# An adaLN block in fp32: down weights asked for earlier, joining sums and the last rows' projection moved

## The chip, the cores and the metric

The kernel runs on one core of a Trainium2 chip. That core has TensorE (PE, with its weight loads shown as PEld), VectorE (DVE), ScalarE (ACT), GpSimd (POOL) and SyncE (SP, here only a queue of DMA requests). All five run their own instruction streams in the order in which they were written down, and wait for one another through semaphores. The metric is device time of one execution in microseconds (us). Before the change the median of three runs is 2881.68 us.

## The reference

One transformer block with adaptive layer norm, in fp32. There are 2048 rows of 576 features, 32 heads of 18 features and a gated feed-forward part of 4608 features.

```python
mod = (silu(c) @ w_mod).reshape(1, 6, 1, -1)
sa, ca, ga, sb, cb, gb = (mod[:, i] for i in range(6))

h = layernorm(x) * (1 + ca) + sa
q, k, v = heads(h @ wqkv)                  # 32 heads of 18
p = softmax(q @ k.T * 18**-0.5)            # 2048 x 2048 for each head
x = x + ga * (merge(p @ v) @ wo)

h = layernorm(x) * (1 + cb) + sb
x = x + gb * ((sigmoid(h @ w_gate) * (h @ w_up)) @ w_down)
```

## The kernel before, in words

**Attention.** The 2048 query rows are two halves. A unit is a pair of heads for one half, so there are 32 units, and each has 16 steps, one for every 128 keys. In a step PE makes four tiles of scores, ACT turns them into exponentials, and PE multiplies these with the values, two steps behind, into one sum bank `o` (L577). Between them PE makes a second set of scores in turns ("m" in the order strings), from which DVE takes the row maxima (L481) that a later unit needs. The maxima run about a unit and a half ahead and end during unit 30. In a paired unit ACT takes over a part of the maxima (L484, L486). In the units listed in `SINGLE` DVE reduces all of them.

The end of a unit is handed on in three places of the next unit. At its step 1 ACT copies the bank `o` into the tile `oT` (L591). At step 3 PE transposes `oT`, DVE takes reciprocals and ACT writes the transposed tile back into `oT` (L616). Then POOL scales it into the output rows `Oa` or `big` (L620). There is one `oT` and one bank `o`, so the copy of the next unit waits until POOL has read the last one, and PE's next values wait for that copy.

**Work beside attention.** Three generators are advanced a piece at a time.

- `down_parts` prepares the 18 blocks of down weights on POOL, from unit 4, step 8 to unit 14, three pieces in four steps. For each block it asks for the weights (L852, a POOL DMA tied to an exponential of that step), scales them by the gate (four L873), makes the sums for a seven-product matrix scheme (L879 to L883), splits everything into a high and a low part (L869, L870, L898, L899) and stores it to DRAM (L892 for the parts, L900 twice for the sums). Two weight tiles alternate.
- `first_rows` projects the first half of the rows, from unit 15 on.
- `last_rows_project` projects the second half in eight groups of 128 rows, from unit 27, step 5 on. Each group takes three turns, one in every second step: transposes, then nine matmuls for each of two column halves (L714), with a DVE addition (L716). Its rows of x arrive by POOL DMA in a tile of the feed-forward pool (`raw1`), where the sums are also made and stored from.

Units 16 to 20 and 27 to 29 run with `SINGLE` maxima. From unit 1 to unit 29 SP asks, at the start of a unit, for the queries and keys of the unit after next (L440 to L448), eight requests.

The order of PE's instructions is written out by hand in all of this. The order on the other engines is set by a planner, which places an instruction where its own estimate says that the engine is free and the inputs are there. It places the code's instructions, and the code's order only breaks ties.

**Feed-forward.** Each half of the rows goes through 18 blocks of 256 hidden features. A block takes seven products, in the order 1, 6, 2, 7, 5, 4, 3, and two half "downs" with the weights prepared above. In the second half, blocks 1 to 16 also use the seven-product scheme for the down part: products go into four tiles `G`, and in the last block eight joining sums (`joined`, L1243) add these to the output. From the seventh product on DVE and ACT keep the code's order too.

Of the kernel before, what the change touches and what calls it, by code (L numbers as in the profile page):

```python
# [15 lines left out]
F32 = mybir.dt.float32  # L16
F32R = mybir.dt.float32r
# [6 lines left out]
P = 128  # L24
S = 2048
D = 576
# [11 lines left out]
HW = S // 2  # L38
UNITS = H
LEAD = 6  # L40
FROM0, FROM1 = 15 * 16, 27 * 16 + 5
DL = 384
ORDER = (1, 6, 2, 7, 5, 4, 3)
LOOK = 4
# [1 line left out]
NB = F // 256  # L46
LAG = 2

MAXIMA = ((1, 0), (0, 0), (1, 1), (0, 2), (1, 2), (0, 3), (0, 1), (1, 3))
SINGLE = (0, 1, 16, 17, 18, 19, 20, 27, 28, 29)  # L50
FIRST = ((0, 0), (1, 0), (0, 2), (0, 1), (1, 1), (1, 2), (0, 3), (1, 3))
STARTS = tuple(range(2, 15))
STARTED = ((0, 0), (0, 1), (1, 1), (1, 0)), ((0, 0), (0, 1), (1, 0), (1, 1))
# [10 lines left out]
def tile_block(ctx, tc, x_in, wqkv, wo, w_gate, w_up, w_down, c_in, w_mod, out):  # L64
# [351 lines left out]
    def temp(shape, dtype):  # L416
        temps["n"] += 1
        return qpool.tile(shape, dtype, name=f"t{temps['n'] % 2}")
# [213 lines left out]
    def load_wo():  # L632
# [31 lines left out]
        for _ in range(4):  # L664
            yield

    def project_o(t):

        wo_h, wo_l, we = weights
        T, T_ = temp([P, 2048], F32R), temp([P, 2048], F32)  # L670
        xt, full, od = T_[:, 0:D], T_[:, 1024:1536], T_[:, 1536:1664]
        if t >= 8:
            xt = raws.tile([P, 2, 3, 256], F32, name="raw1", bufs=2).rearrange("p v t c -> p (v t c)")[:, 0:D]
        nc.gpsimd.dma_start(xt, x_rows[:, t, :])
        src = Os[t // 8][:, t % 8, :]
        n = 4 if t < 8 else DL // P
        oh = T[:, 0 : n * P]
        ol = T[:, 512 : 512 + n * P]
        pt = bank()
        for i in range(n):  # L680
            nc.tensor.transpose(pt[:, i * P : (i + 1) * P], src[:, i * P : (i + 1) * P], ident)
        if t >= 12:
            nc.vector.tensor_copy(oh, pt[:, 0 : n * P])
            nc.vector.tensor_sub(ol, pt[:, 0 : n * P], oh.bitcast(F32))
        else:
            full = full[:, 0 : n * P]
            nc.vector.tensor_copy(full, pt[:, 0 : n * P])
            nc.gpsimd.tensor_copy(oh, full)
            nc.gpsimd.tensor_sub(ol, full, oh.bitcast(F32))
        yield  # L690
        if t < 8:
            om = T[:, 1024:1152]
            omh = T[:, 1152:1280]
            nc.gpsimd.tensor_copy(
                od.rearrange("p (a e) -> p a e", e=64), src[:, DM:D].unsqueeze(1).to_broadcast([P, 2, 64])
            )
            pt = bank()
            nc.tensor.transpose(pt[:, 0:P], od, ident)
            nc.vector.tensor_copy(od, pt[:, 0:P])
            nc.gpsimd.tensor_copy(om[0:64], od[0:64])  # L700
            nc.gpsimd.tensor_copy(omh[64:P], od[64:P])
            nc.gpsimd.tensor_sub(om[64:P], od[64:P], omh[64:P].bitcast(F32))
            yield
        for h in range(2):
            cols = slice(h * HALF, (h + 1) * HALF)
            ts_ = []
            for i in range(n):
                a, b = oh[:, i * P : (i + 1) * P], ol[:, i * P : (i + 1) * P]
                ts_ += [(a, wo_h[:, i, cols]), (a, wo_l[:, i, cols]), (b, wo_h[:, i, cols])]
            if t < 8:  # L710
                ts_ += [(om, we[:, 0, cols]), (om, we[:, 1, cols])]
            acc = bank()
            for i, (a, w) in enumerate(ts_):
                nc.tensor.matmul(acc[:, :HALF], a, w, start=i == 0, stop=i == len(ts_) - 1)  # L714
            to = Oa[:, t, :] if t < 8 else xt
            nc.vector.tensor_add(to[:, cols], xt[:, cols], acc[:, 0:HALF])  # L716
            yield
        if t >= 8:
            nc.gpsimd.dma_start(x1p[:, t - 8, :], xt)
# [128 lines left out]
    def down_parts():  # L848
# [9 lines left out]
        ahead = load(0)  # L858
        yield
        yield  # L860
        for b in range(NB):
            t = ahead
            hi, lo = t[:, 0 : 2 * D], t[:, 2 * D : 4 * D]
            raw = lo.bitcast(F32)
            quads = [slice(i * HALF, (i + 1) * HALF) for i in range(4)]
            b11, b12, b21, b22 = (raw[:, q] for q in quads)

            def split(i):
                nc.gpsimd.tensor_copy(hi[:, quads[i]], raw[:, quads[i]])  # L869
                nc.gpsimd.tensor_sub(lo[:, quads[i]], raw[:, quads[i]], hi[:, quads[i]].bitcast(F32))  # L870

            for i, q in enumerate(quads):
                nc.gpsimd.tensor_mul(raw[:, q], raw[:, q], gb_b[:, i % 2 * HALF : (i % 2 + 1) * HALF])  # L873
                if i == 2:
                    yield
            if b < SEVENS:
                two = [temp([P, 2048], F32R) for _ in range(2)]
                (t1, t2), (t3, t4) = ([x[:, (2 + i) * HALF : (3 + i) * HALF].bitcast(F32) for i in range(2)] for x in two)
                nc.gpsimd.tensor_sub(t1, b12, b11)  # L879
                nc.gpsimd.tensor_sub(t3, b22, b12)  # L880
                yield
                nc.gpsimd.tensor_sub(t2, b22, t1)
                nc.gpsimd.tensor_sub(t4, t2, b21)  # L883
            if b + 1 < NB:
                ahead = load(b + 1)
            yield
            split(0)
            split(1)
            yield
            split(2)  # L890
            split(3)
            nc.gpsimd.dma_start(wds[b].bitcast(F32), t[:, 0 : 4 * D].bitcast(F32))  # L892
            yield
            if b < SEVENS:
                for i, x in enumerate(two):
                    for k in range(2):
                        to, part = x[:, k * HALF : (k + 1) * HALF], x[:, (2 + k) * HALF : (3 + k) * HALF]
                        nc.gpsimd.tensor_copy(to, part.bitcast(F32))  # L898
                        nc.gpsimd.tensor_sub(part, part.bitcast(F32), to.bitcast(F32))  # L899
                    nc.gpsimd.dma_start(  # L900
                        wtd[b, :, 2 * D * i : 2 * D * (i + 1)].bitcast(F32), x[:, 0 : 2 * D].bitcast(F32)
                    )
                    yield
# [558 lines left out]
    for n, (hf, b, k) in enumerate(seq):  # L1462
# [72 lines left out]
        if k == 1:  # L1535
# [6 lines left out]
            flush()  # L1542
            if hf and not b:
                second_half()
        elif k == 6:
            st["b_"] = banks()
            product(st, 6, st["b_"], True)
# [44 lines left out]
                behind.append(got)  # L1592
        if hf and not b and k in (4, 3):
            load_columns(0, {4: 2, 3: 4}[k])
        if hf and b == NB - 1:
            for i in {1: (0, 1), 2: (2, 3), 5: (4,), 4: (5, 6), 3: (7,)}.get(k, ()):
                joined(i)
        if before is not None and k == 6:
            down(before, 0, {3: lambda: weights_low(n + 2)})
        elif before is not None and k == 7:  # L1600
            down(before, 1, {3: lambda: weights_low(n + 2), 5: lambda: weights_low(n + 3), 7: lambda: weights_low(n + 4)})
        elif k in (6, 7):
            for i in (2,) if k == 6 else (2, 3, 4):
                weights_low(n + i)
# [56 lines left out]
```

## Time and profile before

| | |
|---|---|
| median of three runs | 2881.68 us (2878.94 to 2881.8) |
| the profiled execution | 2879.64 us, span 2877.8 us |
| granted PE clock, mean | 0.996 |
| attention, units 0 to 31 | 242.8 to 1601.3 us of the span |
| feed-forward | 1606.2 us to the end |

A profile lists, for each engine, when it was busy and what ended its idle time. PE is busy for 98% of the span, and this counts matmuls whose ends are modelled, so it doesn't mean that PE could not do more. The lines that carry the argument are shown with the prediction. In a timeline a row gives start, length, engine, line, operation, tiles written and read, shapes and how many instructions were merged. The bracket holds the engine's idle time before it and what ended that.

### The profile page before, as it was taken

What the parts mean: (1) busy time and instruction counts of PE and PEld (TensorE: products, weight loads), DVE (VectorE), ACT (ScalarE), POOL (GpSimd) and SP (SyncE); (2) the same over time, 40 slices, a digit from 0 to 9 for tenths busy, and PEclk for the clock granted to TensorE, in tenths of its full rate; (3) what the DMA queues carried; (4) which work ended last, traced back from release to release, by engine and by line L of the source; (5) the groups of instructions that cost most, each with busy time, mean ns of one, the idle gap of its engine ahead of it and who ended that gap; (6) DMA issues with size and microseconds to landing.
All of it is one profiled execution on the core that took longest, in us unless ns stands there. A gap on an engine that the chain in (4) does not pass through costs nothing.

```text
span 2877.8 us, 46834 instructions
## 1 busy us (share of the span) xinstructions
PE 2820.3 (98%) x16885; PEld 1855.6 (64%) x16885; DVE 2336.0 (81%) x4367; ACT 1591.6 (55%) x2989; POOL 821.3 (29%) x1089
## 2 busy tenths in 40 slices
PE   7999999999999999999999999999999999999998
PEld 5974444443434444444444688888888888888888
DVE  7287888888889998999985588887888687777776
ACT  2215899999988778998778522334333222222221
POOL 3125307776763111555012322232222100000000
PEclk9999999999999999999999999999999999999999
DMA  5444214444442111222124766667776966665653
GB/s 168 127 148 132 69 49 149 143 159 164 168 151 80 57 35 49 75 95 78 52 65 124 260 230 238 226 225 252 277 263 237 381 198 200 199 199 198 199 197 109
DMA packets 170104, 462.33 MB, mean 161 GB/s; under 512 B 21196, under 2 KB 87760, under 8 KB 159760
## 3 DMA queue, kind: packets, MB, share of 16 engines
q1 hardware_dynamic: 148768, 358.36, 37.0%
q0 software_dynamic: 21104, 100.98, 9.9%
q8 instruction: 133, 2.18, 0.3%
q14 instruction: 99, 0.81, 0.1%
HBM read 281.92 MB, written 176.82 MB: 159 GB/s over the span
## 4 chain that ended last, share of the span: by engine, by line
PE 83%; POOL 6%; DVE 4%; issue 3%; ACT 2%; DMA 1%; SPq 0%; POOLq 0%; ACTq 0%; DVEq 0%
PE x L1113 26%; PE o L577 14%; PE s L475 10%; PE s L985 10%; PE d L1263 8%; PE d L1195 6%; PE s L300 4%; PE s L714 2%; PE s L351 2%; ACT p L989 2%; POOL w L870 1%; POOL t L899 1%; DVE mx L481 1%; POOL w L873 1%; PE s L601 1%
## 5 line engine op out<-in xcount | busy, mean ns | idle before, releaser
L481 DVE TENSOR_REDUCE mx<-s 128x1 f32<-128x512 f32 x1696 | 1076.7, 684 | 128.5 <-PE s L475 110.2
L989 ACT ACTIVATE p<-s 128x512 f32<-128x512 f32 x2048 | 1068.7, 610 | 143.8 <-PE s L475 73.7
L475 PE MATMUL s<-k,q 54*128 54x512 f32 x1920 | 607.6, 451 | 8.3 <-ACT p L989 1.8
L577 PE MATMUL o<-p,vaug 128*32 128x512 f32 x4096 | 555.4, 608 | 6.9 <-ACT oT L591 6.5
L985 PE MATMUL s<-q,k 56*128 56x512 f32 x1920 | 555.4, 426 | 1.7 <-DVE mx L481 0.6
L985 PEld LDWEIGHTS s<-q,k 56*128 56x128 f32 x1920 | 264.9, 186 | 293.3 <-DVE mx L481 177.3
L475 PEld LDWEIGHTS s<-k,q 54*128 54x128 f32 x1920 | 272.8, 185 | 250.4 <-ACT p L989 150.4
L1113 PE MATMUL x<-k,w 128*128 128x512 f32 x1512 | 369.7, 392 | 2.4 <-ACT w L1094 2.4
L1113 PEld LDWEIGHTS x<-k,w 128*128 128x128 f32 x1512 | 278.3, 189 | 54.6 <-ACT w L1094 2.6
L1263 PE MATMUL d<-wd,hh 128*128 128x288 f32 x1280 | 256.7, 295 | 3.8 <-DVE Oa L1267 3.7
L1113 PE MATMUL x<-w,w 128*128 128x512 f32 x1008 | 245.1, 391 | 0.0
L1113 PE MATMUL x<-big,w 128*128 128x512 f32 x1008 | 244.3, 391 | 0.0
L1263 PEld LDWEIGHTS d<-wd,hh 128*128 128x128 f32 x1280 | 207.2, 188 | 8.7 <-DVE Oa L1267 5.1
L1113 PEld LDWEIGHTS x<-big,w 128*128 128x128 f32 x1008 | 185.3, 188 | 35.4 <-DVE u L1569 0.3
L1113 PEld LDWEIGHTS x<-w,w 128*128 128x128 f32 x1008 | 184.4, 188 | 34.3
L577 PEld LDWEIGHTS o<-p,vaug 128*32 128x32 f32 x4096 | 83.5, 108 | 169.3 <-issue 146.3
L1263 PE MATMUL d<-wd,hl 128*128 128x288 f32 x640 | 189.1, 295 | 1.6 <-DVE hl L1142 1.6
L1267 DVE TENSOR_TENSOR Oa<-Oa,d 128x288 f32<-128x288 f32 x320 | 139.9, 453 | 55.6 <-PE d L1263 51.7
L1271 POOL DMA_DIRECT2D out_dram<-Oa x16 | 8.7, 545 | 583.1 <-DVE Oa L1267 583.1
L1122 ACT ACTIVATE sg<-x 128x512 f32<-128x512 f32 x36 | 21.6, 599 | 209.1 <-PE x L1113 209.1
L1094 ACT CAST w<-S 128x768 fp32r<-128x768 f32 x72 | 60.1, 835 | 134.9 <-POOL S L1072 133.4
L1124 ACT ACTIVATE u<-u 128x512 f32<-128x512 f32 x72 | 45.5, 632 | 145.6 <-DVE u L1508 93.3
(262 smaller groups left out, 4052.6 us busy)
## 6 DMA issues: line engine op xcount, KB each, us to landing
ws<-w SPq DMA_DIRECT2D x126, 640.0 KB
w<-ws SPq DMA_DIRECT2D x126, 640.0 KB
wd<-wds SPq DMA_DIRECT2D x19, 1152.0 KB
k<-kd SPq DMA_DIRECT2D x60, 360.0 KB
wds<-w POOLq DMA_DIRECT2D x18, 1152.0 KB, 4.7
wtd<-t POOLq DMA_DIRECT2D x32, 576.0 KB, 4.3
wt<-wtd SPq DMA_DIRECT2D x64, 288.0 KB
wd<-wds SPq DMA_DIRECT2D x52, 288.0 KB
```

Source lines behind the costliest of these rows:

```text
L300: nc.tensor.matmul(acc, w, hT[:, t, cols], start=n == 0, stop=n == len(ts_) - 1)
L351: nc.tensor.matmul(acc[:, 0:HALF], hT[:, k, rows], w, start=n == 0, stop=n == len(ts_) - 1,)
L475: nc.tensor.matmul(sp, qs[rows, qt * P : (qt + 1) * P], ks[rows, at * 512 : (at + 1) * 512], start=True, stop=True,)
L481: nc.vector.tensor_reduce(to, sp, axis=AX.X, op=ALU.max)
L577: nc.tensor.matmul(acc[32 * j : 32 * j + 32, :], vaug[:, kt, (2 * p + h) * VW : (2 * p + h) * VW + 32], probs[2 * c + h], start=kt == 0, s ...
L985: nc.tensor.matmul(sT, ks[rows, kcols], qs[rows, c * 512 : (c + 1) * 512], start=True, stop=True)
L989: state["exp"] = nc.scalar.activation(pr, sT, AF.Exp, scale=SCALE)
L1094: nc.scalar.copy(w[:, :, 0:3, :], src)
L1113: nc.tensor.matmul(acc[v], w[:, v, a, :], X[s][:, b, :], start=first and n == 0, stop=n == 6, skip_group_check=not first,)
L1195: nc.tensor.matmul(acc, a[:, rows], w[:, k, :], start=n == 0, stop=n == 2)
L1263: nc.tensor.matmul(acc[:, :HALF], a[:, f, rows], w[:, f, cols], start=n == 0, stop=n == 5)
L1267: nc.vector.tensor_add(Oa[:, t, cols], Oa[:, t, cols], acc[:, :HALF])
```

## The change

There are three edits.

1. In `down_parts` the next block's weights are asked for after the third scaling of the current block, one piece of the generator earlier than before (there the request followed the sums).
2. `FROM1` moves from unit 27, step 5 to unit 28, step 9, and unit 27 leaves `SINGLE`. From the ninth group on (`t >= 8`) the projection holds one pair of tiles, and each group uses one half of them in turn, for the x rows too, so `raw1` is no longer used here.
3. The joining sums of the last block are written inside turns 1, 6 and 7: two in product 1, three behind the first down half of product 6, three behind the second one of product 7. Before, they stood in turns 1, 2, 5, 4 and 3.

```diff
-FROM0, FROM1 = 15 * 16, 27 * 16 + 5
+FROM0, FROM1 = 15 * 16, 28 * 16 + 9
...
-SINGLE = (0, 1, 16, 17, 18, 19, 20, 27, 28, 29)
+SINGLE = (0, 1, 16, 17, 18, 19, 20, 28, 29)
...
+    held_rows = []
+
     def project_o(t):
...
-        T, T_ = temp([P, 2048], F32R), temp([P, 2048], F32)
-        xt, full, od = T_[:, 0:D], T_[:, 1024:1536], T_[:, 1536:1664]
-        if t >= 8:
-            xt = raws.tile([P, 2, 3, 256], F32, name="raw1", bufs=2).rearrange("p v t c -> p (v t c)")[:, 0:D]
+        if t <= 8:
+            held_rows[:] = temp([P, 2048], F32R), temp([P, 2048], F32)
+        T, T_ = held_rows
+        if t < 8:
+            xt, full, od = T_[:, 0:D], T_[:, 1024:1536], T_[:, 1536:1664]
+        else:
+            T, T_ = T[:, 1024 * (t % 2) : 1024 * (t % 2) + 1024], T_[:, 960 * (t % 2) : 960 * (t % 2) + 960]
+            xt, full = T_[:, 0:D], T_[:, D : D + 384]
         nc.gpsimd.dma_start(xt, x_rows[:, t, :])
...
                 if i == 2:
                     yield
+                    if b + 1 < NB:
+                        ahead = load(b + 1)
...
-            if b + 1 < NB:
-                ahead = load(b + 1)
             yield
...
             if hf and not b:
                 second_half()
+            if hf and b == NB - 1:
+                for i in (0, 1):
+                    joined(i)
...
-        if hf and b == NB - 1:
-            for i in {1: (0, 1), 2: (2, 3), 5: (4,), 4: (5, 6), 3: (7,)}.get(k, ()):
-                joined(i)
         if before is not None and k == 6:
             down(before, 0, {3: lambda: weights_low(n + 2)})
+            if hf and b == NB - 1:
+                for i in (2, 3, 4):
+                    joined(i)
         elif before is not None and k == 7:
             down(before, 1, {3: lambda: weights_low(n + 2), 5: lambda: weights_low(n + 3), 7: lambda: weights_low(n + 4)})
+            if hf and b == NB - 1:
+                for i in (5, 6, 7):
+                    joined(i)
```

What this does to the order is told here at three places. Lines behind the edits carry numbers that are 6, 8 or more higher in the new kernel: L852 is L858, L873 is L879, L892 is L898, L898 is L904, L899 is L905, L900 is L906, L1243 is L1249.

The first place is POOL at the end of down block 0, in unit 5. The tiles `w` are the block's weights, `t` its sums. Before:

```order
L892 DMA wds<-w_4801 128x2304
L898 CAST t_4939<-t_4939 128x288
L898 CAST t_4940<-t_4940 128x288
L899 TENSOR_TENSOR t_4939<-t_4939 128x288
L899 TENSOR_TENSOR t_4940<-t_4940 128x288
L900 DMA wtd<-t_4939 128x1152
L852 DMA w_4982<-in_B_w_down_dram 128x2x576
L898 CAST t_4940<-t_4940 128x288
L899 TENSOR_TENSOR t_4940<-t_4940 128x288
L900 DMA wtd<-t_4940 128x1152
L873 TENSOR_TENSOR w_4982<-w_4982,gb_b 128x288 x4
```

And in the changed kernel:

```order
L898 DMA wds<-w_4801 128x2304
L858 DMA w_4938<-in_B_w_down_dram 128x2x576
L904 CAST t_4941<-t_4941 128x288
L904 CAST t_4942<-t_4942 128x288
L905 TENSOR_TENSOR t_4941<-t_4941 128x288
L905 TENSOR_TENSOR t_4942<-t_4942 128x288
L906 DMA wtd<-t_4941 128x1152
L904 CAST t_4942<-t_4942 128x288
L879 TENSOR_TENSOR w_4938<-w_4938,gb_b 128x288
L905 TENSOR_TENSOR t_4942<-t_4942 128x288
L879 TENSOR_TENSOR w_4938<-w_4938,gb_b 128x288
L906 DMA wtd<-t_4942 128x1152
```

The load of block 1 moved ahead of two casts, two subtractions and one store. For every later block the load stands straight before its four multiplications in both kernels.

The second place is POOL in down block 10, at the start of unit 11. `Oa<-oT,rec` is the scaling of unit 9's outputs, which unit 11's first ACT copy waits for. Before:

```order
L852 DMA w_8161<-in_B_w_down_dram 128x2x576
L873 TENSOR_TENSOR w_8161<-w_8161,gb_b 128x288 x4
L879 TENSOR_TENSOR t_8459<-w_8161 128x288
L880 TENSOR_TENSOR t_8460<-w_8161 128x288
L882 TENSOR_TENSOR t_8459<-w_8161,t_8459 128x288
L869 CAST w_8161<-w_8161 128x288
L620 TENSOR_TENSOR Oa<-oT,rec 128x8x18 x2
L883 TENSOR_TENSOR t_8460<-t_8459,w_8161 128x288
```

And in the changed kernel, from the same cast on:

```order
L875 CAST w_8130<-w_8130 128x288
L891 TENSOR_TENSOR t_8462<-t_8461,w_8130 128x288
L876 TENSOR_TENSOR w_8130<-w_8130 128x288
L875 CAST w_8130<-w_8130 128x288 x2
L876 TENSOR_TENSOR w_8130<-w_8130 128x288 x2
L875 CAST w_8130<-w_8130 128x288
L904 CAST t_8461<-t_8461 128x288
L876 TENSOR_TENSOR w_8130<-w_8130 128x288
L905 TENSOR_TENSOR t_8461<-t_8461 128x288
L898 DMA wds<-w_8130 128x2304
L620 TENSOR_TENSOR Oa<-oT,rec 128x8x18 x2
```

The scaling moved behind the store of the block's parts. In block 15, at the start of unit 14, it moved likewise from right behind the parts' store to behind the first store of sums.

The third place is DVE in the last block, from the second down half of turn 7 on. `Oa<-Oa,G` are the joining sums, `u<-x,u` and `p<-x,p` read the products 5 and 4, and `hl<-p,hh` is the low part that the last down needs. Before:

```order
L1267 TENSOR_TENSOR Oa<-Oa,d 128x288 x8
L1569 TENSOR_TENSOR u_32841<-x,u_32841 128x512 x2
L1132 TENSOR_TENSOR u_32841<-u_32841 128x512
L1243 TENSOR_TENSOR Oa<-Oa,G_27449 128x4x288
L1142 TENSOR_TENSOR hl_27566<-u_32841,hh_27565 128x512
L1580 TENSOR_TENSOR p_32713<-x,p_32713 128x512 x2
L1132 TENSOR_TENSOR p_32713<-p_32713 128x512
L1243 TENSOR_TENSOR Oa<-Oa,G_27449 128x4x288
L1243 TENSOR_TENSOR Oa<-Oa,G_27447 128x4x288
L1142 TENSOR_TENSOR hl_27564<-p_32713,hh_27563 128x512
L1586 TENSOR_TENSOR u_32737<-x,u_32737 128x512 x2
L1243 TENSOR_TENSOR Oa<-Oa,G_27447 128x4x288
```

And in the changed kernel:

```order
L1273 TENSOR_TENSOR Oa<-Oa,d 128x288 x8
L1249 TENSOR_TENSOR Oa<-Oa,G_27435 128x4x288
L1249 TENSOR_TENSOR Oa<-Oa,G_27433 128x4x288 x2
L1578 TENSOR_TENSOR u_32828<-x,u_32828 128x512 x2
L1138 TENSOR_TENSOR u_32828<-u_32828 128x512
L1148 TENSOR_TENSOR hl_27552<-u_32828,hh_27551 128x512
L1589 TENSOR_TENSOR p_32699<-x,p_32699 128x512 x2
L1138 TENSOR_TENSOR p_32699<-p_32699 128x512
L1148 TENSOR_TENSOR hl_27550<-p_32699,hh_27549 128x512
L1595 TENSOR_TENSOR u_32723<-x,u_32723 128x512 x2
```

The joins moved together, ahead of everything that reads products 5, 4 and 3. In turn 6 three of them likewise stand behind the first down half, ahead of turn 2's gate.

## The prediction

> **What bounds the kernel now.** I read the page's header and chain first, then the waits, then the busy times unit by unit, then timelines of POOL, SP and DVE at the places that the change touches.
>
> ```profile
> span 2877.8 us, 46834 instructions
> PE 2820.3 (98%) x16885; PEld 1855.6 (64%) x16885; DVE 2336.0 (81%) x4367; ACT 1591.6 (55%) x2989; POOL 821.3 (29%) x1089
> PE 83%; POOL 6%; DVE 4%; issue 3%; ACT 2%; DMA 1%; SPq 0%; POOLq 0%; ACTq 0%; DVEq 0%
> ```
>
> PE carries the chain, yet POOL, busy for 29%, has 6% of it. The next rows are windows cut at the first exponential of attention units 9, 11, 14, 15, 26, 27, 28, 29, the first ten and last six steps of unit 30, and unit 31. The columns are the length, then busy time on PE, PEld, DVE, ACT and POOL, clock, DMA share, GB/s.
>
> ```profile
> 610.38:650.23 39.85, 39.58 (x264) 16.34 (x264) 35.75 (x68) 37.93 (x77) 33.67 (x55) 1.00 0.41 146
> 690.04:734.10 44.06, 41.41 (x264) 16.92 (x263) 36.11 (x69) 38.10 (x77) 35.23 (x59) 0.96 0.48 170
> 813.71:860.94 47.23, 42.68 (x261) 17.25 (x261) 37.86 (x69) 36.09 (x72) 29.49 (x50) 0.93 0.45 159
> 860.94:902.30 41.36, 41.12 (x262) 17.08 (x260) 39.72 (x66) 34.09 (x68) 19.27 (x23) 1.00 0.30 88
> 1346.48:1388.02 41.54, 41.44 (x261) 17.41 (x260) 40.22 (x67) 34.10 (x68) 0.82 (x2) 1.00 0.12 38
> 1388.02:1432.89 44.87, 44.58 (x305) 20.28 (x304) 42.22 (x73) 34.53 (x68) 5.63 (x10) 1.00 0.19 57
> 1432.89:1479.32 46.43, 46.43 (x317) 21.48 (x315) 41.98 (x77) 35.86 (x70) 6.73 (x12) 1.00 0.25 72
> 1479.32:1526.64 47.32, 47.32 (x319) 22.94 (x316) 40.20 (x79) 38.09 (x75) 4.11 (x8) 1.00 0.20 61
> 1526.64:1554.34 27.70, 27.18 (x181) 12.02 (x180) 23.68 (x45) 24.29 (x47) 7.15 (x12) 1.00 0.51 173
> 1554.34:1566.98 12.64, 12.46 (x74) 3.94 (x73) 0.32 (x2) 12.14 (x26) 4.59 (x7) 1.00 0.69 145
> 1566.98:1601.29 34.31, 33.90 (x196) 10.91 (x195) 0.26 (x1) 33.18 (x67) 4.01 (x7) 1.00 0.38 131
> ```
>
> An undisturbed paired unit takes 39.85 us, with PE and ACT both close to full. Units 11 and 14 are longer, at a lower mean clock. With single maxima and no projection a unit takes 41.36 or 41.54 us (DVE at about 40). With projection and PE full it takes 47.32. In unit 31 the maxima are over: 68 matmuls fewer than in unit 9, DVE idle, ACT busy for 33.18 of 34.31. ACT sets the pace there and PE has room, whatever its modelled ends say.
>
> **Down weights.** The waits say why units 11 and 14 are long (first row: whole run; then the two units' starts).
>
> ```profile
> POOL w L873 <- DMA w<-in_B_w_down_dram: 106.9, 18, 11.8
> PE o L577 <- ACT oT L591: 2.4, 1, 2.4
> PE o L577 <- ACT oT L591: 4.1, 1, 4.1
> ```
>
> ```profile
> 693.83 0.81 POOL L620 TENSOR_TENSOR Oa<-oT,rec 128x144 f32<-128x144 f32 x2
> 694.67 0.59 ACT L591 COPY oT<-o 128x512 f32<-128x512 f32 x1 [2.57 <-POOL Oa L620]
> 812.56 0.81 POOL L883 TENSOR_TENSOR t<-t,w 128x288 f32<-128x288 f32 x1
> 818.58 0.58 POOL L892 DMA_DIRECT2D wds<-w  x1
> 819.18 0.82 POOL L620 TENSOR_TENSOR Oa<-oT,rec 128x144 f32<-128x144 f32 x2
> ```
>
> POOL does a unit's output scaling (L620) between pieces of down blocks. When it comes to it late, ACT can't reuse oT, the sum bank stays full, and PE stops. The clock then falls as well:
>
> ```profile
> 695.45:698.90 3.45, 3.45 (x19) 1.38 (x18) 1.60 (x3) 3.45 (x8) 3.45 (x7) 0.62 0.55 170
> ```
>
> Today's price: unit 11 44.06 - 39.85 = 4.2 us; unit 14 47.23 less 40.5 (nine steps at the paired rate, seven at unit 15's), 6.7. Together 10.9 us, of which 6.5 are the gaps and 4.4 the slow restart (1.8 and 2.6).
>
> The change moves the request in the code, but POOL's written order shows what comes of it. Only block 1's load moves ahead of other work; from block 2 on each load still stands straight before its own multiplications, so the 106.9 us of waiting stay POOL's own. Two things do change. First, block 1's load is asked for some 3 us earlier and no longer queues behind a sums store. Second, the scaling stands later: in block 10 behind the store of the parts instead of before L883, 6.6 us of POOL work later (812.56 to 819.16 are the same pieces), and in block 15 five pieces later, about 2.8 (the same kinds of pieces as above: two casts, two subtractions, a store). Alone the second is a loss, so the outcome hangs on how long each load then waits. That depends on the next unit's keys (the first request of units 7, 8, 10 and 13, on SP):
>
> ```profile
> 465.22 1.56 POOL L873 TENSOR_TENSOR w<-w,gb_b 128x288 f32<-128x288 f32 x2 [9.34 <-DMA w<-in_B_w_down_dram]
> 527.86 0.79 SPq L440 DMA_DIRECT2D q<-qd  x1
> 540.94 1.56 POOL L873 TENSOR_TENSOR w<-w,gb_b 128x288 f32<-128x288 f32 x2 [11.00 <-DMA w<-in_B_w_down_dram]
> 568.61 0.79 SPq L440 DMA_DIRECT2D q<-qd  x1
> 588.30 0.80 POOL L873 TENSOR_TENSOR w<-w,gb_b 128x288 f32<-128x288 f32 x1 [6.46 <-DMA w<-in_B_w_down_dram]
> 648.28 0.79 SPq L440 DMA_DIRECT2D q<-qd  x1
> 664.90 1.56 POOL L873 TENSOR_TENSOR w<-w,gb_b 128x288 f32<-128x288 f32 x2 [11.79 <-DMA w<-in_B_w_down_dram]
> 733.90 1.56 POOL L873 TENSOR_TENSOR w<-w,gb_b 128x288 f32<-128x288 f32 x2 [3.63 <-DMA w<-in_B_w_down_dram]
> 771.94 0.79 SPq L440 DMA_DIRECT2D q<-qd  x1
> 783.93 1.56 POOL L873 TENSOR_TENSOR w<-w,gb_b 128x288 f32<-128x288 f32 x2 [8.60 <-DMA w<-in_B_w_down_dram]
> ```
>
> These are blocks 1, 4, 6, 9, 12 and 14. A load issued 1 to 4 us behind the first key request (start of L873 less wait less 0.7) waits 8.6 to 11.8 us; one at 12.5 us behind, 6.5; one clear of the keys, 3.6. Walk forward. Block 2 begins 2.9 us early: block 1's load is asked for those two casts, two subtractions and a store sooner. (An estimate; it would be 0 if the keys of unit 5 still hold that load until 465.2, and over 4 if the missing store counts too.) Block 3's load comes some 15 us behind unit 6's keys, between the cases of 6.5 and 3.6, and I let it lose 0.6. So block 4's load goes out about 1 us ahead of unit 7's keys and I take a wait of 5 for its 11.0: 8 ahead. Block 6's load then meets unit 8's keys 5 us after their start, 11.5 for 6.5: 3 ahead. Block 9's load stands 1.2 behind unit 10's keys, as block 4's does today: 11.0 for 11.8, 3.6 ahead. Block 10's scaling is then 6.6 - 3.6 = 3.0 late on today: gap 2.4 + 3.0 = 5.4, and 2.6 for the restart, 8.0 us. Unit 13 thereby starts 3.8 later, block 14's load falls ahead of its keys (4 for 8.6), and the scaling in block 15 is due in time: 819.18 + 2.8 - 5.8 = 816.2 against 815.6 + 3.8. No second stall. This term: 8.0 - 10.9 = -2.9. Its ends: -10.9 (no stall left) and +12.3 (two stalls of 9.0, no advance at all).
>
> **Projection from unit 28, unit 27 paired.** The same 24 turns move 20 steps later. Unit 27 falls from 44.87 to that of 15 and 26, 41.45: -3.4. Unit 28: nine steps at 41.45/16, seven at 47.32/16, 44.0: -2.4. Unit 29 keeps 47.32. Unit 30's first ten steps go from 27.70 to 29.6 (47.32 x 10/16): +1.9. Its last six take 18 matmuls and unit 31 takes 27, at
>
> ```profile
> 2828.41 6.36 PE d L1263 x48
> ```
>
> 6.36/48 = 0.13 us each, so 2.4 and 3.6 us of PE work where ACT sets the pace; I charge 0.4 and 0.6 for bursts that hold up scores. If that cover fails the whole 6.0 shows. Unit 27's maxima, made in units 25 and 26, lose eight DVE reductions to eight ACT ones: 41.45 to about 40.5, -1.0. Sum: -3.9. Ends: -7 (nothing charged, unit 27 at the paired rate) and +1.6 (below). Own input buffers: x rows no longer share raw1, so the first gate and up loads need not wait; those are early today, so nothing.
>
> Each third of rows also issues POOL DMAs, an x row's load and a sum's store, and some now stand behind the twelve paced loads of unit 30, the last of which is
>
> ```profile
> 1557.64 0.73 POOL L919 DMA_DIRECT2D raw<-in_B_w_up_dram  x1
> ```
>
> Twelve such issues are 8.8 us of POOL's queue. The one x load behind them belongs to the last rows, whose first addition comes 14 steps later, some 30 us at unit 31's rate: nothing. POOL's scaling for unit 30 stands behind two stores and their additions; it has until a unit later. What is late next: two operand loads (L938) now wait for the last projection, seven steps (15 us) before attention's end, and are needed in the third product, some 11 us after it. Nothing shows there unless a load takes over 25 us.
>
> **Joins.**
>
> ```profile
> 2856.27 2.62 DVE L1243 TENSOR_TENSOR Oa<-Oa,G 128x1152 f32<-128x1152 f32 x2
> 2858.80 0.68 DVE L1142 TENSOR_TENSOR hl<-p,hh 128x512 fp32r<-128x512 f32 x1
> 2859.54 0.40 PE L1263 MATMUL d<-wd,hl 128*128 128x288 f32 x1 [1.59 <-DVE hl L1142]
> 2860.61 1.35 DVE L1243 TENSOR_TENSOR Oa<-Oa,G 128x1152 f32<-128x1152 f32 x1
> 2862.37 0.53 PE L1263 MATMUL d<-wd,hh 128*128 128x288 f32 x2 [0.84 <-DVE Oa L1267]
> ```
>
> The joins sit before what PE waits for, twice. Moved behind the earlier down products they free 1.27 us each there. But three in a row now delay product 5's sums by 2.6 us; passed down the row hl<-p ends near 2858.7 instead of 2859.5. So of 1.59 some 0.8 goes and of 0.84 all: -1.6. Ends -2.4 and -0.8.
>
> **Sum.** -2.9 - 3.9 - 1.6 = -8.4 us. The profiled execution was 2879.64 us (span 2877.8), 2.0 below the median of the three runs, 2881.68; against that median I forecast 2873.3.
>
> **Rivals.** (1) Block 4's load gains nothing by going first, since the keys overtake it. For: no row lies between 2.4 us ahead (3.63) and 1.3 behind (11.00). Then about 1 us of advance is left at block 10, the gap is 8.0 plus 2.6, and unit 14 is spared by the shift: 10.6 for 10.9, sum -5.8, 2875.9. [...] (2) Block 9's load slips ahead of unit 10's keys too, 1.2 us more: the advance becomes 10, both stalls go, -10.9 - 3.9 - 1.6 = -16.4, 2865.3. (3) Slower: no advance reaches block 10, and two of blocks 11 to 14 that wait about 4 today meet keys (11 to 11.8). Both units then stall 9.0, 23.2 for 10.9, sum +6.8, 2888.5. It decides once POOL has lost 9.5 us between units 11 and 14. Against: today only block 14 meets keys there, and a longer unit 11 moves keys away. (4) The projection isn't hidden: unit 30's first ten steps hold two matmul turns and 2.8 us over ten paired steps, 1.4 each; eight such turns, 11.2 us, make that term +1.6, sum -2.9, 2878.8.
>
> **Chances.** Forecast 0.46, (1) 0.22, (2) 0.16, (3) 0.08, (4) 0.08. A change of 0.2% (5.8 us) is about what a measurement of this kernel can tell. Faster by more: most of the forecast (0.39), half of (1), all of (2): 0.66. Slower: (3), 0.08. Same: the rest, 0.26. The forecast's own range is 2869 to 2877; with (1), most of (2) and (4) it is 2864 to 2881.
>
> **What would show it.** Right: L873 waits for block 4 near 5 and block 6 near 11; an ACT wait for L620 of about 5.5 us at unit 11 and none at unit 14; unit 27 near 41.5, unit 31 under 35.5; the gap before hl at the end near 0.8, the next gone. Wrong: an ACT wait at unit 14, or at two other units; unit 30 over 45; a wait of the first products for operand loads.

## The result and the profile after

The changed kernel took 2878.47 us (median of 22 runs, 2873.56 to 2887.26), the kernel before, run beside it, 2885.22 (22 runs, 2877.94 to 2892.21). The ratio is 0.9978 with a 95% interval of 0.997 to 0.9987, that is 6.3 us faster (3.8 to 8.7). A second measurement (e6 below) gave 0.9983 (0.9975 to 0.9992), 4.9 us faster. The forecast was 8.4 us faster, 2873.3 us. The sign held, and 2878.47 lies in the wide range (2864 to 2881) but outside the forecast's own (2869 to 2877); the kernel before was itself 3.5 us above the median that the forecast started from. Of the three terms one came out right, one was oversized by a factor of 3.5, and one can't be told from nothing.

The first rows are from the page of the changed kernel.

```profile
span 2874.6 us, 46836 instructions
PE 2817.3 (98%) x16885; PEld 1855.8 (65%) x16885; DVE 2335.0 (81%) x4367; ACT 1595.5 (56%) x2997; POOL 820.6 (29%) x1089
PE 82%; POOL 6%; issue 4%; DVE 3%; DMA 2%; ACT 2%; SPq 0%; POOLq 0%; DVEq 0%; ACTq 0%
```

POOL still has its 6% of the chain. The next rows are windows of the changed kernel: units 11 and 14, then 26 to 31, with the columns of the prediction's table.

```profile
687.85:738.23 50.38, 42.12 (x264) 16.99 (x263) 36.11 (x69) 38.16 (x77) 40.33 (x66) 0.90 0.42 150
817.86:858.06 40.20, 40.03 (x261) 16.69 (x261) 37.25 (x68) 35.88 (x72) 20.71 (x36) 1.00 0.39 133
1344.90:1385.27 40.37, 39.83 (x261) 16.49 (x261) 37.23 (x68) 35.98 (x73) 0.81 (x2) 1.00 0.13 40
1385.27:1426.83 41.56, 41.46 (x261) 17.35 (x260) 40.20 (x67) 34.08 (x68) 0.93 (x3) 1.00 0.14 38
1426.83:1470.15 43.32, 43.12 (x287) 18.62 (x286) 40.00 (x71) 35.48 (x70) 4.97 (x9) 1.00 0.18 53
1470.15:1518.46 48.31, 48.31 (x326) 23.20 (x322) 39.64 (x77) 38.33 (x76) 7.23 (x13) 1.00 0.20 58
1518.46:1562.19 43.73, 43.73 (x288) 19.55 (x287) 27.48 (x54) 36.33 (x72) 12.86 (x20) 1.00 0.46 124
1562.19:1599.02 36.83, 36.42 (x225) 13.93 (x225) 2.74 (x6) 33.63 (x66) 6.18 (x11) 1.00 0.59 212
```

Unit 14's stall is gone (40.20 us for 47.23), but unit 11's has grown, 50.38 for 44.06. Unit 27 fell as it should, to 41.56, but unit 31 rose to 36.83, and it is full of PE work. The waits of the whole run, and POOL and ACT at unit 11:

```profile
PE o L577 <- ACT oT L591: 8.0, 1, 8.0
POOL w L879 <- DMA w<-in_B_w_down_dram: 112.5, 18, 11.9
```

```profile
685.00 3.09 POOL L879 TENSOR_TENSOR w<-w,gb_b 128x288 f32<-128x288 f32 x4 [4.78 <-DMA w<-in_B_w_down_dram]
...
696.65 0.58 POOL L898 DMA_DIRECT2D wds<-w  x1
697.25 0.82 POOL L620 TENSOR_TENSOR Oa<-oT,rec 128x144 f32<-128x144 f32 x2
698.11 0.59 ACT L591 COPY oT<-o 128x512 f32<-128x512 f32 x1 [8.19 <-POOL Oa L620]
```

POOL begins block 10 at 685.00, works through it, stores it at 696.65 and only then scales unit 9's outputs. ACT waits 8.19 us for that. POOL's waits for the down loads did not shrink: 112.5 us for 106.9.

One execution can be split at the first exponentials of units 0, 16 and 25 and at the end of attention (us):

| | before | after | difference |
|---|---|---|---|
| up to attention | 242.79 | 240.43 | -2.36 |
| units 0 to 15 | 659.51 | 659.17 | -0.34 |
| units 16 to 24 | 403.35 | 404.83 | +1.48 |
| units 25 to 31 | 295.64 | 294.59 | -1.05 |
| after attention | 1276.55 | 1275.59 | -0.96 |

The first and third rows hold nothing that the change touches. In the eleven profiled executions of the experiments below attention started anywhere from 241.0 to 243.9 us, and unit 20 took 47.3, 48.8 or 50.2 (the last section shows why). So two single spans cannot be subtracted here; stages and medians can.

### The profile page after: what moved, and what is told of

It is laid out like the page before. It is cut to its first block, busy times and chain, and to the rows that moved or that the text cites. A ratio compares the mean times of both kernels' runs of the same rounds, so it can differ in the third digit from the quotient of the medians.

```text
span 2874.6 us, 46836 instructions
## 1 busy us (share of the span) xinstructions
PE 2817.3 (98%) x16885; PEld 1855.8 (65%) x16885; DVE 2335.0 (81%) x4367; ACT 1595.5 (56%) x2997; POOL 820.6 (29%) x1089
## 4 chain that ended last, share of the span: by engine, by line
PE 82%; POOL 6%; issue 4%; DVE 3%; DMA 2%; ACT 2%; SPq 0%; POOLq 0%; DVEq 0%; ACTq 0%
PE x L1119 25%; PE o L577 14%; PE s L991 10%; PE s L475 10%; PE d L1269 7%; PE d L1201 6%; PE s L300 4%; PE s L351 2%; PE s L720 2%; ACT p L995 2%; DMA out_dram<-Oa 1%; POOL w L876 1%; DVE mx L481 1%; POOL t L905 1%; POOL w L879 1%
## 5 line engine op out<-in xcount | busy, mean ns | idle before, releaser
L484 ACT ACTIVATE over<-s 128x512 f32<-128x512 f32 x184 | 110.3, 599 | 36.4 <-PE s L475 31.9
```

Of the source, the lines that this page charges most:

```text
L484: nc.scalar.activation(over, sp, AF.Relu)
```

## The experiments

### One edit at a time (e1, e2, e3)

e1 is the kernel before with this edit alone:

```diff
                 if i == 2:
                     yield
+                    if b + 1 < NB:
+                        ahead = load(b + 1)
...
-            if b + 1 < NB:
-                ahead = load(b + 1)
```

> Edit 1 alone (the next block's down load asked for inside the current block), projection and joins as before. Theory, revised on the changed kernel's profile: block 1's load gains some 3 us, block 4's load waits 10 to 11 us whether it goes ahead of the keys or behind them, so the scaling of block 10 comes late and unit 11 shows one stall of 10 us, unit 14 none: attention units 0 to 15 within 1 us of before, total 0 to -1 us. Rival (the prediction's size): the stall at unit 11 is 8.0 us, total -2.9 us. Rival (POOL falls back): stalls at two units, total +5 or more.

Measured: 2882.14 us, ratio 0.9997 (0.9987 to 1.0007). Its window of unit 11:

```profile
689.04:739.82 50.78, 42.53 (x264) 17.03 (x263) 36.12 (x69) 38.15 (x76) 40.58 (x67) 0.90 0.42 149
```

The same picture as in the changed kernel: one stall of 8.00 us at unit 11, none at unit 14 (40.22 us), units 0 to 15 together 659.11 for 659.51. Edit 1 alone makes this change of shape, and no gain that a measurement can tell from none.

e2 is the kernel before with the projection's start, the shorter list of single units and the own buffers:

```diff
-FROM0, FROM1 = 15 * 16, 27 * 16 + 5
+FROM0, FROM1 = 15 * 16, 28 * 16 + 9
...
-SINGLE = (0, 1, 16, 17, 18, 19, 20, 27, 28, 29)
+SINGLE = (0, 1, 16, 17, 18, 19, 20, 28, 29)
```

> Edit 2 alone (last rows' projection from unit 28, unit 27 paired, own input buffers). Theory, revised: units 25 to 31 together lose about 1 us, since the 12 turns that now lie in units 30 and 31 are not covered there: unit 30 near 43.7 and unit 31 near 36.8 us. Rival (the prediction): these units lose 3.9 us, with unit 30 near 42.6 and unit 31 near 34.9. Units 11 and 14 keep both stalls, 44 and 47 us, in either case.

Measured: 2884.29 us, ratio 1.0007 (0.9995 to 1.002). Units 30 and 31, and a stretch in unit 11:

```profile
1518.61:1562.33 43.72, 43.72 (x288) 19.56 (x287) 27.48 (x54) 36.32 (x72) 12.83 (x20) 1.00 0.45 124
1562.33:1599.16 36.83, 36.42 (x225) 13.94 (x225) 2.73 (x6) 33.61 (x66) 6.19 (x11) 1.00 0.58 212
```

```profile
699.53:709.77 10.24, 10.24 (x41) 4.02 (x39) 5.58 (x10) 6.31 (x13) 9.64 (x17) 0.50 0.49 195
```

Units 25 to 31 take 294.54 us, 1.1 under the kernel before, unit by unit as in the changed kernel: the size repeats to 0.1 us. The expectation that both stalls stay was wrong. Unit 14 has none in this execution (40.22 us), and unit 11 has a gap of 3.35 us yet is 8.3 us long over its 39.85; the third row shows why: the clock stood at half for 10.24 us.

e3 is the kernel before with the joins moved:

```diff
-            for i in {1: (0, 1), 2: (2, 3), 5: (4,), 4: (5, 6), 3: (7,)}.get(k, ()):
-                joined(i)
...
+                for i in (0, 1):
+                    joined(i)
...
             down(before, 0, {3: lambda: weights_low(n + 2)})
+            if hf and b == NB - 1:
+                for i in (2, 3, 4):
+                    joined(i)
```

and so on with 5, 6 and 7 behind product 7's.

> Edit 3 alone (joining sums of the last block spread over its first products). Theory: after attention nothing changes but the last block, by 0.8 to 1.6 us, the two PE gaps of 1.59 and 0.84 us near the end going to at most 0.8 together. Total -0.8 to -1.6 us. Rival: the DVE sums delayed by the three joins in a row cost what is gained, total 0.

Measured: 2880.52 us, ratio 0.9994 (0.9985 to 1.0003). The waits on PE at the end of the changed kernel, where e3 shows the same idle times:

```profile
2856.69 0.53 PE L1269 MATMUL d<-wd,hh 128*128 128x288 f32 x2 [0.63 <-ACT hh L1143]
2857.42 0.40 PE L1269 MATMUL d<-wd,hl 128*128 128x288 f32 x1 [0.20 <-DVE hl L1148]
```

The gaps of 1.59 and 0.84 us became 0.63 and 0.20: 1.6 us less. The whole stage after attention says the same: it takes 1277.3 us on average in the four profiled executions without edit 3 (before, e1, e2, e5: 1276.55 to 1278.25) and 1275.6 in the nine with it (1274.88 to 1276.52). In e3's unit 11 a gap of 2.06 us stands with another stretch at half clock:

```profile
695.50:705.74 10.24, 10.24 (x41) 4.10 (x39) 5.61 (x10) 6.31 (x13) 9.65 (x17) 0.50 0.59 226
```

By the ratios the three edits alone give -0.9, +2.0 and -1.7 us, each with an interval of some 3 us to either side. Their sum says nothing against 6.3 and nothing for it. What was needed was a kernel without the scatter.

### Taking POOL out of attention's way (e4, e5, e6)

e4 is the changed kernel with this in `outputs`, ahead of the ACT copy:

```diff
+        if not half and 2 <= p <= 14:
+            for h in range(2):
+                f0 = (2 * p + h) * DH
+                nc.vector.tensor_tensor(
+                    Os[half][:, :, f0 : f0 + DH].rearrange("p (c b) e -> p c b e", c=2),
+                    tq[:, 2 * h : 2 * h + 2, :, 0:DH],
+                    rec[:, 2 * h : 2 * h + 2, :].unsqueeze(3).to_broadcast([P, 2, 4, DH]),
+                    op=ALU.mult,
+                )
+            return
         nc.scalar.copy(oT, tp.rearrange("p b q -> p (b q)"))
```

> The changed kernel, with the output scaling of attention units 2 to 14 on DVE straight from the transposes' bank in place of an ACT copy and two POOL multiplications; the down loads stay as in the changed kernel. Theory (POOL, late through its loads, holds ACT's tile, and that alone stalls unit 11): no stall in any unit, POOL's load waits unchanged at 80 us or more in sum, unit 11 near 39.9 us, total 10 us under the changed kernel, if DVE, busy for 35.8 of 39.85 us in a paired unit, has room for 1 us more. Rival (DVE is full): the paired units grow by 0.5 us or more each, and 13 of them take back 6 us or more. Rival (PE's stall has another cause): unit 11 stays over 45 us.

Measured: 2868.22 us (5 runs, 2865.17 to 2868.77), ratio 0.9947 (0.9934 to 0.996). Unit 11, and POOL's waits:

```profile
690.14:730.00 39.86, 39.61 (x262) 16.25 (x261) 36.10 (x70) 37.38 (x76) 33.74 (x54) 1.00 0.47 169
```

```profile
POOL w L889 <- DMA w<-in_B_w_down_dram: 115.9, 18, 13.9
```

POOL waits for its loads as long as ever, and no unit stalls. Units 0 to 15 take 648.46 us for 659.17. DVE is not too full: it is busy for 36.10 of unit 11's 39.86 us, and the paired units keep their length. So the stall is POOL's lateness at the scaling (e8 below leaves the scaling on POOL, makes POOL earlier, and has no stall either), and this version beats both kernels. Its five runs lie within 3.6 us; those of the changed kernel spread over 13.7 (22 runs) and 6.5 (the 12 of e6).

e5 is the kernel before with the same lines and no other edit.

> The kernel before with the output scaling of units 2 to 14 on DVE, as in e4, and none of the three edits. Without POOL in attention's way the two stalls and their scatter go, so the distance to e4 is what edits 2 and 3 are worth with no stall in the way. Theory: -1.1 for edit 2 and -1.2 for edit 3, so this kernel takes 2.3 us more than e4 (2870.5), with repeats as close together as e4's. Rival (the prediction's -3.9 and -1.6): 5.5 us more, 2873.7. Its distance to the kernel before is what the stalls cost there: theory 12 us, more than the 10.9 that one execution showed.

Measured: 2870.54 us (6 runs), ratio 0.9959 (0.9945 to 0.9974). Its distance to e4, 2.3 us, is the one expected of edits 2 and 3 by their stages (e4 ran in another session; the kernel before took 2882.74 us there and 2882.90 here). In the two profiled executions units 25 to 31 differ by 0.5 us and the stage after attention by 1.9. Its distance to the kernel before, 12.4 us, is what the stalls cost there at the median. But the repeats lie 11.3 us apart (2866.80 to 2878.09), not as close as e4's, and the profile does not tell why. The 2.3 is therefore no sharp number.

> The changed kernel again beside the others, unchanged. Theory: one stall, at unit 11, of 8 to 11 us, unit 14 without one; 10 us over e4's kernel, near 2878. Rival (the gain of 6 us is scatter between sessions): within 3 us of the kernel before.

Measured: 2878.68 us (12 runs), ratio 0.9983. The profiled execution's unit 11:

```profile
691.99:742.61 50.62, 41.29 (x264) 16.95 (x263) 36.12 (x69) 38.16 (x77) 41.45 (x67) 0.90 0.42 149
```

Again one stall at unit 11, none at unit 14 (40.20), 10.5 us over e4. The changed kernel pays 10.5 for its one stall where the kernel before paid 12.4 for its two: edit 1 is worth some -1.9 by medians, -0.3 in the one pair of executions, and e1's interval (-3.7 to +2.0) holds both and nothing. The profiled executions even lean the other way: units 0 to 15 took 659.5, 658.7 and 655.9 us with the old order (before, e2, e3) and 659.2, 659.1 and 660.1 with the new one (after, e1, e6). Whether edit 1 gains anything stays open.

### Where a turn of the projection costs (e7, e9)

e7 is e4's kernel with the projection's old start, and unit 27 still paired:

```diff
-FROM0, FROM1 = 15 * 16, 28 * 16 + 9
+FROM0, FROM1 = 15 * 16, 27 * 16 + 5
```

> e4's kernel with the projection back at its old start (unit 27, step 5), and unit 27's maxima still paired. Theory: the projection's turns cost the same wherever they lie, so only the pairing is worth something; units 27 to 31 return to 44.9, 46.4, 47.3, 40.3 and 34.3, units 25 and 26 stay at 40.4, and the sum of 25 to 31 is 294.1, 0.7 under e4's 294.8. Rival (the prediction): moving the projection is worth 2.9 us, so this is 2.9 us slower than e4.

Measured: 2870.19 us, ratio 0.9958 (0.9945 to 0.9971). Unit 27:

```profile
1375.38:1423.57 48.19, 48.09 (x303) 21.96 (x302) 43.11 (x73) 34.71 (x67) 5.62 (x10) 1.00 0.16 50
```

My theory failed: units 25 to 31 took 297.53 us, not 294.1. Unit 27's six turns, which cost 3.3 us in the kernel before (44.87 less 41.54), cost 7.8 when unit 27 is paired (48.19 less 40.4). A turn costs about 1.3 us in a paired unit and 0.56 in a single one. The maxima made in unit 27 are those of units 28 and 29, single in both kernels; what unit 27 itself gets by leaving `SINGLE` is the paired units' order of PE's instructions, and PE is busy for 48.09 us there for 44.58, for about as many matmuls (303 for 305). Why the turns cost more in that order is not shown. So the two parts of edit 2 need each other. The rival's number (2.9) nearly came out (2.7 by these units, 2.0 by the medians), but not for its reason: it was to come from the old place of the turns, and it comes from turns in a paired unit.

e9 moves the start eight steps earlier instead:

```diff
-FROM0, FROM1 = 15 * 16, 28 * 16 + 9
+FROM0, FROM1 = 15 * 16, 28 * 16 + 1
```

> e4's kernel with the projection eight steps earlier, from unit 28, step 1, so that four turns move from unit 31 to unit 28 and unit 31 has none. Theory (a turn costs 0.5 to 0.9 us wherever it stands, since PE is full in unit 31 too): unit 31 falls from 37.1 to 34.3, unit 28 grows from 43.3 to about 46.4, units 25 to 31 together 294.6 to 295.2 against e4's 294.8, no change in the total. Rival (unit 31 alone lacks cover, turns in unit 28 are cheaper): the sum falls by 1 us or more.

Measured: 2868.20 us, ratio 0.9941 (0.9928 to 0.9953). Units 28 and 31:

```profile
1420.16:1466.40 46.24, 46.24 (x317) 21.73 (x316) 41.49 (x75) 35.80 (x71) 7.69 (x13) 1.00 0.22 66
1558.69:1593.00 34.31, 33.82 (x195) 10.82 (x195) 0.26 (x1) 33.18 (x66) 4.59 (x9) 1.00 0.59 215
```

Unit 31 without turns is back at 34.31, unit 28 pays 2.9 us for the four that it got, and units 25 to 31 take 295.22 for 294.84. Four turns cost 2.8 us in unit 31 (37.12 in e4 less 34.31) and 2.9 in unit 28 (46.24 less 43.33). Units 29 and 30 changed by -1.1 and +1.3, since some turns with matmuls moved from one to the other (319 matmuls for 326, 296 for 288). Unit 31 has no more cover than unit 28.

### What makes a down load slow (e8)

e8 is the changed kernel with fewer loads of queries and keys:

```diff
-        if 0 < u < UNITS - 2:
+        if 0 < u < UNITS - 2 and not 7 <= u + 2 <= 13:
             load_heads(u + 2)
```

> The changed kernel without the queries' and keys' loads of attention units 7 to 13, which therefore compute with older keys. Theory (a down load is slow when it is asked for just behind a unit's keys): the loads of blocks 4, 6, 9, 12, 13 wait as the others do, 4.5 to 6 us from issue to the first multiplication instead of 6.4 to 12.7; POOL reaches block 10's scaling some 17 us earlier, and unit 11 takes 39.9 us with no stall; total about 10 us under the changed kernel. Rival (the loads are slow for another reason, such as the stores of sums in front of them): their times stay, unit 11 keeps 50 us.

Measured: 2866.68 us (4 runs), ratio 0.9943 (0.9928 to 0.9959), 12.0 us under the changed kernel beside it (e6). Block 4's load takes 5.33 us to the first multiplication where it took 11.55, block 9's 4.74 for 12.68, and POOL asks for block 10 at 660.6 us for 679.5. Block 13's took 14.67 us, against the expectation: POOL's lead had brought it 4.5 us behind the request for unit 14's keys (made at unit 12's start, as each unit asks for the keys of the unit two later), which this kernel still makes. POOL comes to unit 11 early enough:

```profile
684.20:724.30 40.10, 39.85 (x267) 16.39 (x264) 36.02 (x69) 38.03 (x76) 30.72 (x50) 1.00 0.33 120
```

The keys make the loads slow: with them taken away, the loads of blocks 4 and 9 are quick (5.33 and 4.74 us). Across all ten profiled executions of kernels with all their keys and the paced loads (blocks 1 to 15, 150 loads), the time from a load's issue to its first multiplication goes by where it stands against the nearest unit's first key request:

| load issued | loads | us, least / median / most |
|---|---|---|
| 1 to 3 us ahead of the keys | 16 | 4.4 / 5.1 / 6.4 |
| less than 1 us ahead | 5 | 4.7 / 6.7 / 7.5 |
| less than 1 us behind | 4 | 7.0 / 9.0 / 10.9 |
| 1 to 9 us behind | 33 | 9.4 / 12.2 / 14.6 |
| 9 to 17 us behind | 20 | 5.1 / 7.1 / 7.9 |
| clear of them (over 3 us ahead, or 17 behind) | 72 | 4.5 / 5.4 / 6.9 |

Ten of the 33 are block 1's, whose time holds 2 to 3 us of POOL's own work; without them the row is 9.4 / 12.5 / 14.6.

Block 4 shows both sides. In the changed kernel its load stands 1.2 us behind unit 7's first request; in e7 1.4 us ahead:

```profile
525.32 0.79 SPq L440 DMA_DIRECT2D q<-qd  x1
```

```profile
526.52 0.73 POOL L858 DMA_DIRECT2D w<-in_B_w_down_dram  x1
538.07 2.33 POOL L879 TENSOR_TENSOR w<-w,gb_b 128x288 f32<-128x288 f32 x3 [10.82 <-DMA w<-in_B_w_down_dram]
```

```profile
525.95 0.73 POOL L868 DMA_DIRECT2D w<-in_B_w_down_dram  x1
531.13 1.58 POOL L889 TENSOR_TENSOR w<-w,gb_b 128x288 f32<-128x288 f32 x2 [4.46 <-DMA w<-in_B_w_down_dram]
```

```profile
527.33 0.79 SPq L440 DMA_DIRECT2D q<-qd  x1
```

The first two fences are the changed kernel's SP and POOL, the last two e7's POOL and SP. Going first by 1.4 us saves 6.4.

### Loads that really go ahead (e10, e11)

The words of edit 1 come true if the loads are not tied to an exponential. e10 does that to e4's kernel, e11 to the changed kernel, whose scaling is on POOL:

```diff
-            paced(nc.gpsimd.dma_start(
+            nc.gpsimd.dma_start(
```

> e4's kernel with the down loads no longer tied to an exponential. In POOL's order each load then stands ahead of the third or fourth multiplication of the block before it, as edit 1's words have it. Theory: POOL's waits for these loads fall from 112 us to under 30 and its last block ends 80 us or more earlier, yet the total stays within 2 us of e4's 2868, since nothing waits for POOL there any more. Rival (the loads' waits still reach attention in another way): 3 us or more faster than e4.

Measured: 2868.78 us (4 runs), ratio 0.994 (0.9925 to 0.9955). No wait for a down load is left; what POOL waits for instead is a free buffer (POOL's waits from 430 to 900 us):

```profile
POOL w L868 <- DMA wds<-w: 26.4, 8, 3.7
```

Its last store of the blocks ends at 754.9 us for 857.2 in e4. POOL gained 102 us and the kernel none that can be told: 2868.78 us for 2868.22, or 2 us by the ratios, whose intervals overlap.

> The changed kernel (scaling on POOL) with the down loads not tied to an exponential. The order then has the loads ahead, but places the scalings by a POOL that it takes to be quicker: those of units 7, 8 and 9 stand behind blocks 11, 14 and 17. Theory (not the loads' own waits but how many POOL blocks stand ahead of a unit's scaling decides): even at 18 us a block with no waits POOL comes to them some 36, 50 and 60 us late, so attention stalls in several units and the total is 50 to 80 us above the changed kernel. Rival (the loads' waits were the whole trouble): no stall at unit 11, 10 us under the changed kernel.

Measured: 2933.39 us (one run). The waits:

```profile
PE o L577 <- ACT oT L591: 58.1, 3, 22.1
```

Units 8, 9 and 10 take 62.01, 64.41 and 58.20 us, 64.9 more than in the changed kernel, and unit 11, at 40.08, takes 10.3 less; that makes up the 55 us of this one run. With the waits for loads gone altogether the wait is 58.1 us for the 8.0 of the changed kernel, since the order now places each scaling behind more blocks. The stalls came a unit earlier than expected: it was the scalings of units 6, 7 and 8, behind blocks 8, 11 and 14, that came late, while that of unit 9, behind block 17, came in time. What stands ahead of the scaling decides, not how long the loads take by themselves.

## Why the prediction came out as it did

- **Down weights, -2.9 forecast.** Right: the loads stay POOL's own waits; the scaling comes later and unit 11 pays for it; the shift of the later units spares unit 14, with block 14's load ahead of its keys (a wait of 4.16 us for 8.60, forecast 4). Wrong: the walk forward along the blocks, at block 4. It had block 2 begin 2.9 us early, block 3's load lose 0.6, and block 4's load go out 1 us ahead of unit 7's keys. Taking out the 2.4 us by which attention began earlier, block 2's load went out 1.9 early, block 3's took 7.03 us for 5.28 (1.75 lost), and block 4's stood 0.3 us early, still 1.2 behind the keys, and waited 10.82. Block 6's wait was 5.79, not 11. So unit 11's wait was 8.19, not 5.5, and its price 10.5, not 8.0. This error of 2.5 and the one of 1.5 in the next point pull the term in opposite ways, so that it still looks near by medians (-1.9) is luck. The price is the size of rival (1), 10.6, but its reason, that the keys overtake a load which went ahead of them, no run shows: here the load was never ahead, and the 16 loads that went 1 to 3 us ahead of the keys took 4.4 to 6.4 us (e8's table), where the 33 that went 1 to 9 us behind them took 9.4 to 14.6.
- **Today's price, 10.9 forecast.** 12.4 at the median (e5), since the kernel before does not always stall as in the execution shown: units 11 and 14 cost 4.2 and 6.7 there (7.0 against the 40.2 that unit 14 took undisturbed in the changed kernel), 8.3 and nothing in e2, 6.9 and 1.5 in e3. The term was worked out from one draw of several.
- **Projection and unit 27, -3.9 forecast, -1.1 measured.** Unit 27 came at -3.3 (forecast -3.4), unit 28 at -3.1 (-2.4), units 25 and 26 at -1.5 (-1.0). The term failed at the three units that receive the turns: unit 29 +1.0 (forecast 0), unit 30 +3.4 (+2.3), unit 31 +2.5 (+0.6). Unit 30's first ten steps took 29.14 us, a little under the forecast's 29.6; its last six, where the maxima are over, 14.59 for 12.64, +1.95 where 0.4 was charged. The step at fault is "ACT sets the pace there and PE has room, whatever its modelled ends say", on which 18 matmuls in those six steps and 27 in unit 31 were charged at 1.0 of their 6.0 us: 4.5 showed. The row said 33.90 busy of 34.31, and e9 shows that it was nearer the truth than ACT's. Unit 29's +1.0 was overlooked: of its eight turns six now hold matmuls, where five did (326 matmuls for 319, an estimated 0.9 us at 0.13 each, from the prediction's row of 48). Not rival (4) either: it charged units 30 and 31 with 8.4 us more (11.2 less the 2.8 that were there), the forecast with 2.9, and they took 5.9. That the measured 2878.47 stands next to rival (4)'s 2878.8 is chance.
- **Joins, -1.6 forecast.** The two gaps lost 1.60 us, and the stage after attention 1.6 on average. That the gap before hl would be 0.8 was right in sum (0.63 and 0.20, now split between hh and hl), and the second gap went.
- **The sum.** -1.9 for the loads by medians, -1.1, -1.6: -4.6, where the two measurements have -6.3 and -4.9. The parts are not resolved more finely than that. Only the joins and the units that lose their turns came as reasoned; that the total came as near as 2.1 us is in part luck.
- **The other rivals.** (2) needed a POOL early enough at block 10: only e8 made it so. (3) did not come: unit 14 was spared in after, e1 and e6. It was spared in e2 as well, which has the old order: there too a long unit 11 had moved what follows.

## What to carry to other kernels

When an engine with a long list of side work also does one small step that the main loop waits for, look at what stands ahead of that step in its written order; take the step to an engine that keeps the loop's pace (here DVE, 10 us) before making the side work quicker, which gave nothing (e10) or lost 55 (e11). Here a move that was to hide work where PE was busy for 99% (33.90 of 34.31 us in unit 31) hid little (of 6.0 us in the last 22 steps 4.5 showed), whatever ACT's row (33.18) seemed to say. Where a wait depends on which of two transfers goes first, a walk over many blocks carries its error from block to block: give the outcome as a lottery with its prices, not as one line.

## What the runs showed that was not expected

In these executions the half-clock stretch after a stall does not follow the stall's length. A gap of 2.40 us was followed by one of 3.41 us in the kernel before, one of 2.06 by 10.24 in e3, one of 3.35 by 10.24 in e2, which began only 1.6 us after the gap had ended; the gap of 8.02 in the changed kernel had 10.24 as well, of which half lay inside the gap:

```profile
693.55:698.75 5.20, 0.00 (x1) 0.01 (x1) 0.00 (x0) 0.64 (x2) 5.18 (x11) 0.50 0.53 182
698.75:703.79 5.04, 5.04 (x23) 1.55 (x23) 1.98 (x3) 3.98 (x8) 4.65 (x8) 0.50 0.68 278
```

A gap of 1.18 us in e3 had none, yet two gaps of 0.46 and 0.65 us in e2's unit 7 were followed by 3.41. The stretches after these gaps, after unit 14's in the kernel before (6.83 us after a gap of 4.08) and in unit 20 below last once, twice or three times 3.41 us. In e11, where three gaps last 58.1 us together (the longest 22.1), the mean clock is 0.986 for the changed kernel's 0.995. So a short gap can cost more than it lasts (e3: 2.06 of gap, 6.9 in all), and a long one less than both together, since the slow stretch then partly falls into the gap: 8.02 of gap, 10.5 in all. That one gap draws one stretch of 3.41 us and another three is not explained by any run here. It is one source of the scatter between executions that stall (unit 11's gap of 2.40 us cost 4.2 in the kernel before, the one of 2.06 cost 6.9 in e3). That it is another source which load meets which keys is my estimate, from loads that took 5.1 us ahead of the keys and 12.2 behind them at the median.

Unit 20 took 47.35, 48.75 or 50.18 us in executions of kernels that do not differ there, in steps of some 1.4 us, and the clock is the reason. In the changed kernel:

```profile
1114.93 0.50 PE L475 MATMUL s<-k,q 54*128 54x512 f32 x2 [1.62 <-DVE mx L481]
1117.60 1.94 PE L577 MATMUL o<-p,vaug 128*32 128x512 f32 x8
```

```profile
1116.81:1120.22 3.41, 3.41 (x18) 1.03 (x16) 2.49 (x9) 2.06 (x4) 0.00 (x0) 0.50 0.00 0
```

All thirteen profiled executions have this gap of 1.62 us in unit 20. In seven no slow stretch follows (47.3 to 47.4 us), in four one of 3.41 us (48.7 to 48.8; here eight value matmuls take 1.94 us where it is 1.07 otherwise), in two one of 6.83 (50.1 and 50.2). The same gap at the same place thus costs nothing, 1.4 or 2.8 us from one execution to the next. What decides which is not shown.
